# Loading q and k in 32x32 blocks and transposing them on VectorE in place of TensorE

## The chip, the cores and the metric

The kernel runs on one core of one Trainium2 chip. The metric is the device time of one execution in microseconds; three runs of the kernel before gave a median of 990.67.

## The reference

Three stages follow each other. Attention has batch 4, 8 heads, 768 positions and 64 values per head; each position sees the first 4 positions (the sinks) and the last 128. Its output, as 3072 tokens of 512 values, passes a linear stage, and then a mixture of 8 experts of which each token takes one.

```
scores = scale * np.matmul(q, k.transpose(0, 1, 3, 2))
keep = is_sink | in_window
...
a = a / (np.sum(a, axis=-1, keepdims=True) + 1e-09)
x = np.matmul(a, v)            # attention
a = x @ w1; b = x @ w2
x = (a * b @ w3) @ w_out       # linear stage; then routing, and one expert per token
```

## The kernel before

The engines are TensorE (PE, with its weight loads as PEld), VectorE (DVE), ScalarE (ACT), GpSimd (POOL) and SyncE (SP), which issues most of the transfers. Every fp32 matrix product is made of three products of a high and a low part.

**Attention** runs over 48 work items, n = 0 to 47: a unit of 256 positions (12 of them) times a pair of heads (4). In this document an item is one n. For each n, `a_load` brings q and k in (two buffers each), `a_tqk` turns them so that the head's values lie on the partitions, `a_scores` makes scores, maximum and exponential for the two halves j = 0 and 1, `a_pt` and `a_skT` transpose the probabilities, and `a_pv` multiplies them with v. `att_stream` writes these steps in five pieces per item: `a_load(n + 2)` is written ahead of `a_scores(n, 0)`, and `a_tqk(n + 1)` between the two scores steps of n.

**What `a_tqk` does.** Four TensorE transposes (L396) write q and k, turned, into one bank of the PSUM pool `ps_t`. ScalarE copies the bank into `qh` (L401) and into the key store `ring` (L402): the high parts. The low parts are the remainders. For the first 8 items (`n < FEW`) TensorE and ScalarE make them; from n = 8 on VectorE does, `ql` on L413 and the low half of `ring` on L415, with one operand from the PSUM bank and one from SBUF. `ps_t` has one bank, shared by `a_tqk`, `a_pt` and the routing counts (L798 to L802).

**The linear stage** (`moe1_stream`) runs in six groups of two units, beside the attention of the units to come. A group has eight steps f: 24 matmuls (L715), the products `g` on VectorE (L722, L725), and six matmuls with the first unit's half (L703). When the eight are done, the second unit's half follows in eight short steps, the "late" part, beside which attention is written more densely. `route` then works out each unit's experts on VectorE, 16 products of rows with a gate row per unit (L776) and some small steps; `xs<-rows` (L795) stores its rows. The last group's tail and the experts (L924, L961) end the program.

**The order** of instructions on each engine is set by a list scheduler at build time, from the order in which the code is written, with a cost model of its own. Each engine then works strictly in that order. A transfer into a buffer waits on SP until the last reader of the buffer is done, and what stands behind it on SP waits too.

Of the kernel before, what the change touches and what calls it, by code (L numbers as in the profile page):

```python
# [9 lines left out]
F32 = DT.float32  # L10
# [4 lines left out]
ACTF = mybir.ActivationFunctionType  # L15
ALU = mybir.AluOpType
# [6 lines left out]
def f32(ap):  # L23
    return ap.bitcast(F32)
# [3 lines left out]
def attention_moe_moe_kernel(ctx, tc, q, k, v, w1, w2, w3, w_out, mod_id, w_gate, mod_bias, e_w1, e_w2, out,  # L28
                             n_sink, window, dbg=None):
    nc = tc.nc  # L30
    B, H, S, D = q.shape
# [3 lines left out]
    UNIT = 256  # L35
    NC = S // UNIT
    NU = B * NC
    NP = H // 2
# [6 lines left out]
    NS = 4  # L45
    KW = 128 + NS
    banded = n_sink == NS and window == 128
    QDIV = float(D) ** 0.5
    FEW = 2 * NP if math.frexp(QDIV)[0] == 0.5 else 0

    const = ctx.enter_context(tc.tile_pool(name="const", bufs=1))
# [14 lines left out]
    ps_t = psum_ctx.enter_context(tc.tile_pool(name="ps_t", bufs=1, space=PSUM))  # L66
# [3 lines left out]
    att = att_ctx.enter_context(tc.tile_pool(name="att", bufs=2, side="right"))  # L70
# [4 lines left out]
    def defer(fn):  # L75
        job = [fn]

        def run():
            if job:
                job.pop()()  # L80

        waiting[1].append(run)
        return run
# [11 lines left out]
    idf = const.tile([128, 128], F32, name="idf")  # L95
# [19 lines left out]
    def consts_early():  # L115
# [5 lines left out]
        nc.vector.tensor_scalar(out=neg_r, in0=idf, scalar1=-1.0, scalar2=None, op0=ALU.mult)  # L121
        nc.vector.tensor_scalar(out=negq_r, in0=idf, scalar1=-QDIV, scalar2=None, op0=ALU.mult)
        nc.gpsimd.memset(tmp, 1.0)
# [216 lines left out]
    nat = {}  # L340
# [4 lines left out]
    def a_load(n):  # L345
        u, p = divmod(n, NP)
        b, c = divmod(u, NC)
        hs = slice(2 * p, 2 * p + 2)
        qn = att.tile([128, 2, 2 * D], F32, tag="qn", bufs=2, name="qn")
        kn = att.tile([128, 2, 2 * D], F32, tag="kn", bufs=2, name="kn")  # L350
        for src, dst in ((q, qn), (k, kn)):
            for j in range(2):
                s0 = c * UNIT + j * 128
                nc.sync.dma_start(out=dst[:, j].rearrange("p (h d) -> p h d", h=2),
                                  in_=src[b, hs, s0:s0 + 128, :].rearrange("h s d -> s h d"))
        nat[n] = (qn, kn)

    def a_load_v(n):
        u, p = divmod(n, NP)
# [23 lines left out]
    def a_tqk(n):  # L383
        u, p = divmod(n, NP)
        b, c = divmod(u, NC)
        qn, kn = nat.pop(n)
        if n < NP:
            ring.append(att.tile([128, 2, 3, KW], F32R, tag=f"ring{p}", bufs=1, name="ring"))
        kr = ring[p]
        s0, s1 = 2 * c % 3, (2 * c + 1) % 3  # L390
        blocks = slice(s0, s1 + 1) if s0 < s1 else slice(s1, s0 + 1, s0 - s1)
        tp = ps_t.tile([128, 4, 128], F32, tag="t", name="tqk")
        for x, src in enumerate((qn, kn)):
            for j in range(2):
                i = j if x == 0 or s0 < s1 else 1 - j
                nc.tensor.matmul(out=tp[:, 2 * x + i], lhsT=src[:, j], rhs=idf, is_transpose=True, start=(x + j == 0),  # L396
                                 stop=(x + j == 2), skip_group_check=True)
        qh = att.tile([128, 2, 128], F32R, tag="qh", bufs=2, name="qh")
        ql = att.tile([128, 2, 128], F32R, tag="ql", bufs=2, name="ql")
        scale = 1.0 / float(D) ** 0.5  # L400
        nc.scalar.activation(out=qh, in_=tp[:, 0:2], func=ACTF.Copy, scale=scale)  # L401
        nc.scalar.activation(out=kr[:, 0, blocks, NS:KW], in_=tp[:, 2:4], func=ACTF.Copy)  # L402

        def low_parts():
            if n < FEW:
                nc.tensor.matmul(out=tp[:, 0:2], lhsT=negq_r, rhs=qh, start=False, stop=True, skip_group_check=True)
                nc.tensor.matmul(out=tp[:, 2:4], lhsT=neg_r, rhs=kr[:, 0, blocks, NS:KW], start=False, stop=True,
                                 skip_group_check=True)
                nc.scalar.activation(out=ql, in_=tp[:, 0:2], func=ACTF.Copy, scale=scale)
                nc.scalar.activation(out=kr[:, 1, blocks, NS:KW], in_=tp[:, 2:4], func=ACTF.Copy)  # L410
                sinks()
                return
            nc.vector.scalar_tensor_tensor(out=ql, in0=tp[:, 0:2], scalar=scale, in1=f32(qh), op0=ALU.mult,  # L413
                                           op1=ALU.subtract)
            nc.vector.tensor_tensor(out=kr[:, 1, blocks, NS:KW], in0=tp[:, 2:4], in1=f32(kr[:, 0, blocks, NS:KW]),  # L415
                                    op=ALU.subtract)
            sinks()

        def sinks():
            if c == 0:  # L420
                nc.gpsimd.tensor_copy(out=kr[:, :, :, 0:NS],
                                      in_=f32(kr[:, :, 0, NS:2 * NS]).unsqueeze(2).to_broadcast([128, 2, 3, NS]))

        stt["low", n] = defer(low_parts)
        stt["q", n] = (qh, ql)

    def a_scores(n, j):
# [38 lines left out]
        def norm():  # L466
            r = st[:, 2]
            nc.vector.tensor_scalar(out=st[:, 1], in0=st[:, 1], scalar1=1.0e-9, scalar2=None, op0=ALU.add)
            nc.vector.reciprocal(out=r, in_=st[:, 1])
            if n < FEW:  # L470
                for h in range(2):
# [57 lines left out]
    def a_pv(n):  # L529
# [11 lines left out]
        for x, (vj, cols, pm) in enumerate(spans):  # L541
            for h in range(2):
# [3 lines left out]
        nc.tensor.matmul(out=xp[:, 0, j0 * 128:256], lhsT=stt["vsk", b][:, p, :], rhs=sk[:, j0 * 128:256],  # L546
                         start=False, stop=n >= FEW, skip_group_check=True)
        xh, xl = xb[:, p, 0, u % 3], xb[:, p, 1, u % 3]
        nc.scalar.activation(out=xh, in_=xp[:, 0], func=ACTF.Copy)
        if n < FEW:  # L550
            nc.tensor.matmul(out=xp[:, 0], lhsT=neg_r, rhs=xh, start=False, stop=True, skip_group_check=True)
# [10 lines left out]
    def att_stream():  # L562
        a_tqk(0); yield
        a_load(1)
        a_load_sinks(0)
        a_vsink(0)
        yield
        for n in range(NN):
            if n + 2 < NN:
                a_load(n + 2)  # L570
            a_scores(n, 0); yield
            if n:
                a_load_v(n)
                a_sk(n - 1); a_pt(n - 1); yield
            if n + 1 < NN:
                a_tqk(n + 1)
            if n:
                a_skT(n - 1)
            yield
            a_scores(n, 1); yield  # L580
            if n:
                a_pv(n - 1)
                att_done[0] = n
                if n % (NP * NC) == 0:
                    a_vsink(n // (NP * NC))
            yield
        a_sk(NN - 1); a_pt(NN - 1); yield
        a_skT(NN - 1)
        a_pv(NN - 1)
        att_done[0] = NN  # L590
        yield
# [413 lines left out]
    def front():  # L1005
# [19 lines left out]
        if banded:  # L1025
            a_load(0)
            a_load_v(0)
# [202 lines left out]
```

## Time and profile before

| | |
|---|---|
| median of three runs | 990.67 us (990.64 to 991.0) |
| the profiled execution | 990.5 us |
| its span, first to last instruction | 988.5 us |
| PE busy | 955.5 us (97%) |
| DVE busy | 634.0 us (64%) |
| ACT busy | 442.1 us (45%) |
| POOL busy | 161.0 us (16%) |
| mean granted TensorE clock | 0.993 |

The profiled execution was 2.0 us longer than its span. Busy time is the union of an engine's instructions. PE's matmuls overlap each other in the records, so the mean duration of one is longer than the distance from one start to the next.

### The profile page before, as it was taken

Reading aid. Unit: us, or ns where it says so; the run is one execution under the profiler, and the core shown is the slowest. Engines: PE = TensorE matmul, PEld = TensorE weight load, DVE = VectorE, ACT = ScalarE, POOL = GpSimd, SP = SyncE. Lnnn points to the kernel's source line nnn. Section 1 sums busy time; section 2 is a strip of 40 time slices with the busy share of each in tenths; the row PEclk is TensorE's granted clock in tenths of the full one; section 3 lists DMA queues with packets and bytes.
Section 4 is the critical chain, followed back from the end, with each engine's and each line's share of the span. In section 5 each row is a group of like instructions: output and inputs, shape, how many; then the busy total and the mean of one; then the engine's idle time right before and its main releaser. Section 6 shows DMA issues by size and latency. Waiting matters only on the chain. (4 is left out here: it accounts for less than half of the span.)

```text
span 988.5 us, 15433 instructions
## 1 busy us (share of the span) xinstructions
PE 955.5 (97%) x5000; PEld 728.4 (74%) x5000; DVE 634.0 (64%) x1913; ACT 442.1 (45%) x1266; POOL 161.0 (16%) x237
## 2 busy tenths in 40 slices
PE   4899999999999999999999999999999999999995
PEld 3667777767776777677767776787888888888884
DVE  7956994599449953995499538939934373443432
ACT  3687763454335433553355335413434334433433
POOL 1111110111112111111111111123130312211010
PEclk9899999999999999999999999999999999999998
DMA  8754724122212221221022210422455465444331
GB/s 255 237 159 137 224 73 124 29 54 62 46 28 46 64 46 25 51 73 42 19 54 69 47 23 10 138 76 55 141 180 115 150 78 167 149 144 135 106 121 51
DMA packets 125409, 93.99 MB, mean 95 GB/s; under 512 B 96711, under 2 KB 105159, under 8 KB 125200
## 3 DMA queue, kind: packets, MB, share of 16 engines
q1 hardware_dynamic: 120560, 80.12, 30.2%
q0 software_dynamic: 4768, 12.88, 4.1%
q8 instruction: 40, 0.66, 0.3%
q14 instruction: 41, 0.34, 0.2%
HBM read 80.14 MB, written 13.09 MB: 94 GB/s over the span
## 5 line engine op out<-in xcount | busy, mean ns | idle before, releaser
L715 PE MATMUL ab<-xb,wab 128*128 128x512 f32 x1152 | 288.5, 397 | 0.0
L715 PEld LDWEIGHTS ab<-xb,wab 128*128 128x128 f32 x1152 | 209.9, 188 | 44.6 <-DVE xb L554 0.2
L961 PE MATMUL x<-w 128*128 128x512 f32 x600 | 141.0, 392 | 0.0
L776 DVE CUSTOM_DVE_ANT_0 junk<-rows,wgb 128x512 bf16<-128x512 f32 x192 | 137.0, 714 | 1.9 <-ACT rows L763 0.5
L703 PE MATMUL x2p<-w3o,gh 128*128 128x512 f32 x384 | 130.1, 416 | 0.5 <-ACT gh L692 0.5
L961 PEld LDWEIGHTS x<-w 128*128 128x128 f32 x600 | 111.6, 188 | 23.1 <-DVE w L201 0.4
L524 POOL TENSOR_SCALAR_AFFINE_SELECT ptp<-ptf 128x512 f32<-128x512 f32 (+1 forms) x96 | 63.6, 687 | 344.9 <-ACT ptf L519 344.9
L463 ACT ACTIVATE P<-sp,st 128x132 f32<-128x132 f32 (+1 forms) x192 | 69.2, 366 | 67.6 <-DVE st L461 62.4
L201 DVE TENSOR_TENSOR w<-wst,w 128x512 fp32r<-128x512 f32 x112 | 71.3, 685 | 10.8 <-ACT w L200 10.8
L703 PEld LDWEIGHTS x2p<-w3o,gh 128*128 128x128 f32 x384 | 65.7, 189 | 16.2 <-ACT gh L692 2.8
L703 PE MATMUL x2p<-w3o,gl 128*128 128x512 f32 x192 | 76.5, 399 | 0.0
L722 DVE TENSOR_TENSOR g<-ab,bs 128x256 f32<-128x256 f32 x48 | 20.3, 423 | 85.6 <-PE tqk L396 49.0
L924 PE MATMUL ab<-w,w 128*128 128x512 f32 x288 | 74.9, 395 | 0.0
L928 DVE SCALAR_TENSOR_TENSOR w<-ab,w 128x512 fp32r<-128x512 f32 x48 | 33.1, 690 | 64.4 <-ACT w L927 64.2
L924 PE MATMUL ab<-w 128*128 128x512 f32 x288 | 73.6, 391 | 0.0
L692 ACT ACTIVATE gh<-g 128x256 fp32r<-128x256 f32 x96 | 39.7, 415 | 73.8 <-DVE g L722 55.7
L200 ACT ACTIVATE w<-wst 128x512 fp32r<-128x512 f32 x112 | 63.3, 628 | 7.4 <-DMA wst<-in_moe_w_dram 7.2
L443 PE MATMUL sp<-ring,qh 64*128 64x264 f32 (+1 forms) x384 | 62.7, 331 | 3.6 <-ACT P L463 3.5
L924 PEld LDWEIGHTS ab<-w,w 128*128 128x128 f32 x288 | 53.9, 188 | 12.4
L924 PEld LDWEIGHTS ab<-w 128*128 128x128 f32 x288 | 54.1, 188 | 12.1
L443 PEld LDWEIGHTS sp<-ring,qh 64*128 64x128 f32 x384 | 37.5, 185 | 34.6 <-issue 15.1
L927 ACT ACTIVATE w<-ab 128x512 fp32r<-128x512 f32 x48 | 28.7, 597 | 71.8 <-PE ab L924 71.4
(201 smaller groups left out, 1430.8 us busy)
## 6 DMA issues: line engine op xcount, KB each, us to landing
wst<-in_moe_w_dram SPq DMA_DIRECT2D x56, 512.0 KB
f64st<-in_moe_w_dram SPq DMA_DIRECT2D x32, 512.0 KB
vn<-in_v_dram SPq DMA_DIRECT2D x128, 64.0 KB
xs<-rows SPq DMA_DIRECT2D x12, 513.0 KB
qn<-in_q_dram SPq DMA_DIRECT2D x96, 64.0 KB
kn<-in_k_dram SPq DMA_DIRECT2D x96, 64.0 KB
f64st<-in_moe_w_out_dram SPq DMA_DIRECT2D x8, 512.0 KB
wgb<-wgt SPq DMA_DIRECT2D x1, 2048.0 KB
```

The costliest lines, as they stand in the source:

```text
L200: nc.scalar.activation(out=hi, in_=src, func=ACTF.Copy)
L201: lo_eng.tensor_tensor(out=lo, in0=src, in1=f32(hi), op=ALU.subtract)
L443: nc.tensor.matmul(out=sp[:, h, 0:nk].rearrange("p (a b) -> p a b", b=KW), lhsT=a[hp, j, :], rhs=kr[hp, b_, blocks, :], start=(i == 0), st ...
L463: nc.scalar.activation(out=P[:, j, h, lo:KW], in_=sp[:, h, lo:KW], func=ACTF.Exp, bias=st[:, 0, h:h + 1], accum_out=st[:, 1, h:h + 1])
L524: nc.gpsimd.affine_select(out=parts[:, a, i0:2].rearrange("p j h q -> p (j h) q"), in_=full[:, 2 * i0:4], pattern=[[0, 4 - 2 * i0], [sign, ...
L692: nc.scalar.activation(out=gh, in_=g, func=ACTF.Copy)
L703: nc.tensor.matmul(out=x2p[t], lhsT=a[:, sl], rhs=b_, start=(f == 0 and i == 0), stop=(f == KF - 1 and i == 2))
L715: nc.tensor.matmul(out=bank[nm].rearrange("p (u t) -> p u t", u=2), lhsT=a, rhs=b_, start=(kk == 0 and i == 0), stop=(kk == KD - 1 and i = ...
L776: nc.vector.tensor_tensor_reduce(out=junk, in0=rows[:, t, 0:DM], in1=wgb[0][:, e, :], scale=1.0, scalar=0.0, op0=ALU.mult, op1=ALU.add, ac ...
L924: nc.tensor.matmul(out=hp, lhsT=a[:, fs], rhs=b_, start=(kk == 0 and i == 0), stop=(kk == KD - 1 and i == 2))
L928: nc.vector.scalar_tensor_tensor(out=h[:, 1], in0=hp, scalar=0.0, in1=f32(h[:, 0]), op0=ALU.max, op1=ALU.subtract)
L961: nc.tensor.matmul(out=op, lhsT=a[:, ts], rhs=b_, start=(f == 0 and i == 0), stop=(f == KF - 1 and i == 2))
```

## The change

From n = 8 on (`BY_PE`), q and k are loaded in blocks. Partition group g (32 partitions) holds 32 of a head's 64 values, and the 256 positions lie in eight blocks of 32 columns. One transfer moves 32 partitions x 8 blocks x 32 values, with runs of 128 bytes; an item takes eight such transfers in place of four with runs of 256 bytes. A VectorE transposition of [128, 512] then turns each 32x32 block in place, and the copies and the low parts read that SBUF tile instead of the PSUM bank. The first eight items are unchanged except for the tile's name.

```
+    BY_PE = 2 * NP
...
+        qk = att.tile([128, 2, UNIT], F32, tag="qk", bufs=2, name="qk")
...
+            for g in range(4):
+                h, d0 = 2 * p + g // 2, g % 2 * 32
+                nc.sync.dma_start(out=qk[g * 32:(g + 1) * 32, x].rearrange("p (b i) -> p b i", i=32),
+                                  in_=src[b, h, c * UNIT:(c + 1) * UNIT, d0:d0 + 32].rearrange("(b s) i -> s b i", s=32))
...
-        tp = ps_t.tile([128, 4, 128], F32, tag="t", name="tqk")
-        for x, src in enumerate((qn, kn)):
-            for j in range(2):
-                i = j if x == 0 or s0 < s1 else 1 - j
-                nc.tensor.matmul(out=tp[:, 2 * x + i], lhsT=src[:, j], rhs=idf, is_transpose=True, start=(x + j == 0),
-                                 stop=(x + j == 2), skip_group_check=True)
...
+        else:
+            nc.vector.transpose(out=qk.rearrange("p x s -> p (x s)"), in_=qk.rearrange("p x s -> p (x s)"))
+            qt, kt = (qk[:, x].rearrange("p (j s) -> p j s", j=2) for x in range(2))
+            if s0 > s1:
+                kt = kt[:, ::-1]
...
+        nc.scalar.activation(out=qh, in_=qt, func=ACTF.Copy, scale=scale)
+        nc.scalar.activation(out=kr[:, 0, blocks, NS:KW], in_=kt, func=ACTF.Copy)
...
-            nc.vector.scalar_tensor_tensor(out=ql, in0=tp[:, 0:2], scalar=scale, in1=f32(qh), op0=ALU.mult,
+            nc.vector.scalar_tensor_tensor(out=ql, in0=qt, scalar=scale, in1=f32(qh), op0=ALU.mult,
                                            op1=ALU.subtract)
-            nc.vector.tensor_tensor(out=kr[:, 1, blocks, NS:KW], in0=tp[:, 2:4], in1=f32(kr[:, 0, blocks, NS:KW]),
+            nc.vector.tensor_tensor(out=kr[:, 1, blocks, NS:KW], in0=kt, in1=f32(kr[:, 0, blocks, NS:KW]),
                                     op=ALU.subtract)
```

Line numbers of the changed kernel are 13 or 14 higher behind these edits: L443 is L456 there, L715 is L728, L776 is L789; the transposition is L407 and the block load L360.

The scheduler makes a new order for the whole program. On PE, in the last step f of the second group, the order before has the item's transposes between the weight products (`ab`) and the transposes of the sinks' probabilities (`skn`):

```order
L715 MATMUL ab<-xb,wab 128x512 x12
L515 MATMUL pt<-idf,P 128x128 x4
L715 MATMUL ab<-xb,wab 128x512 x12
L396 MATMUL tqk<-idf,qn 128x128 x2
L396 MATMUL tqk<-idf,kn 128x128 x2
L499 MATMUL xp<-idf,skn 8x128 x2
```

The changed kernel has at the same place:

```order
L728 MATMUL ab<-xb,wab 128x512 x12
L528 MATMUL pt<-idf,P 128x128 x4
L728 MATMUL ab<-xb,wab 128x512 x12
L512 MATMUL xp<-idf,skn 8x128 x2
L716 MATMUL x2p<-w3o,gh 128x512 x2
```

The two `tqk` rows are gone, and the rest stands as before. Over the program 160 transposes leave PE.

On DVE, at the change from a late part to the next group's first step (the first such place), the order before has an item's two low parts (`ql`, `ring`) next to each other, behind the mask and the maximum of another half (`sp`, `st`):

```order
L455 COPY_PREDICATED sp<-past_i,sp 128x2x128
L475 TENSOR_TENSOR P<-P,st 128x264
L461 TENSOR_REDUCE st<-sp 128x2
L413 SCALAR_TENSOR_TENSOR ql<-tqk,qh 128x256
L415 TENSOR_TENSOR ring<-tqk,ring 128x2x128
L504 TENSOR_TENSOR pskT_107<-xp,pskT_107 8x256
```

The changed kernel has, at the same place, the low parts of one item apart, and the transposition of the next item behind them:

```order
L426 SCALAR_TENSOR_TENSOR ql<-qk,qh 128x256
L481 TENSOR_SCALAR st<-st 128x2
L567 TENSOR_TENSOR xb<-xp,xb 128x256
L482 RECIPROCAL st<-st 128x2
L706 TENSOR_TENSOR gl<-g,gh 128x256
L488 TENSOR_TENSOR P<-P,st 128x264
L468 COPY_PREDICATED sp<-cur_i,sp 128x2x128
L428 TENSOR_TENSOR ring<-qk,ring 128x2x128
L474 TENSOR_REDUCE st<-sp 128x2
L798 TENSOR_REDUCE sm<-wk 128x2
L804 TENSOR_REDUCE sm<-wk 128x2
L407 STREAM_TRANSPOSE qk<-qk 128x512
```

Each item's transposition stands after the low part `ql` of the item two before, whose buffer it uses. In dense attention some 39 rows stand between the two, four products `junk` among them; beside the steps f about ten rows, with one product `g` among them. Routing is moved too: between the eighth `g` of a group and the first of the next, 22, 22, 21 and 22 products `junk` stood in the first four gaps, and 20, 18, 18 and 20 stand there now, with three transpositions in each gap; the rest of the routing stands behind the next one to three `g`, together with one transposition in each of these steps.

On SP, the order before alternates the loads of q, k and v, with the stores `xs` between them:

```order
L354 DMA qn<-in_q_dram 128x2x64 x2
L354 DMA kn<-in_k_dram 128x2x64 x2
L795 DMA xs<-rows 128x2x513
L365 DMA vn<-in_v_dram 128x2x64 x3
L354 DMA qn<-in_q_dram 128x2x64 x2
```

The changed kernel has there:

```order
L360 DMA qk<-in_q_dram 32x8x32 x4
L360 DMA qk<-in_k_dram 32x8x32 x4
L808 DMA xs<-rows 128x2x513
L360 DMA qk<-in_q_dram 32x8x32 x4
L360 DMA qk<-in_k_dram 32x8x32 x4
```

Eight issues stand where four did; the sequence of items and stores is otherwise alike, with some loads of v moved by one place.

## Rows read from the trace of the kernel before

**Rows 1.** The page: engines, and VectorE's busy tenths in 40 slices
```profile
PE 955.5 (97%) x5000; PEld 728.4 (74%) x5000; DVE 634.0 (64%) x1913; ACT 442.1 (45%) x1266; POOL 161.0 (16%) x237
...
DVE  7956994599449953995499538939934373443432
```

**Rows 2.** Busy time by stretch (`x`: instructions): A, late parts
```profile
core 0: us, PE busy (x) PEld busy (x) DVE busy (x) ACT busy (x) POOL busy (x), PEclk, DMA share, GB/s
192.60:231.50 38.90, 37.93 (x222) 25.58 (x220) 36.90 (x133) 22.73 (x86) 4.89 (x10) 1.00 0.26 61
...
494.20:532.80 38.60, 37.63 (x221) 25.50 (x219) 36.82 (x132) 22.81 (x86) 5.04 (x10) 1.00 0.26 62
sum 160.10, PE 156.44 PEld 106.29 DVE 150.09 ACT 94.09 POOL 23.77; mean PE 39.11 PEld 26.57 DVE 37.52 ACT 23.52 POOL 5.94
```

**Rows 3.** The same view: sums of B (three steps f each) and C
```profile
sum 99.80, PE 99.80 PEld 76.85 DVE 75.74 ACT 34.69 POOL 13.81; mean PE 24.95 PEld 19.21 DVE 18.93 ACT 8.67 POOL 3.45
...
sum 141.30, PE 141.30 PEld 109.30 DVE 58.83 ACT 46.89 POOL 22.72; mean PE 35.33 PEld 27.32 DVE 14.71 ACT 11.72 POOL 5.68
```

**Rows 4.** The same view of L396 alone: busy (matmuls), one A, one B
```profile
192.60:231.50 38.90, 2.90 (x20) 1.00 0.26 61
231.50:257.00 25.50, 0.87 (x7) 1.00 0.20 56
```

**Rows 5.** Busy time by stretch, columns as in group 2: ahead of A, and its fullest part
```profile
88.00:150.00 62.00, 61.86 (x353) 45.56 (x354) 58.73 (x134) 42.73 (x123) 8.94 (x16) 1.00 0.52 149
...
200.00:225.00 25.00, 24.08 (x148) 16.19 (x147) 24.56 (x90) 14.25 (x57) 3.40 (x7) 1.00 0.27 61
```

**Rows 6.** Waits from 150 to 608 us: total us, times, longest
```profile
PEld tqk L396 <- ACT ptf L519: 2.4, 7, 0.5
...
PEld tqk L396 <- ACT ptp L521: 1.8, 5, 0.4
```

**Rows 7.** Timeline of PE around one item's four transposes: start, us
```profile
403.65 0.38 PE L396 MATMUL tqk<-idf,qn 128*128 128x128 f32 x2
403.87 0.38 PE L396 MATMUL tqk<-idf,kn 128*128 128x128 f32 x2
404.09 0.38 PE L499 MATMUL xp<-idf,skn 128*8 128x128 f32 x2
```

**Rows 8.** VectorE instructions by line: ns min/median/max; first and last start
```profile
L752 DVE STREAM_TRANSPOSE wgst<-wgst x1: 692/692/692, 145.4 to 145.4; 32x512 f32<-32x512 f32 x1
...
L380 DVE TENSOR_TENSOR vsk<-vst,vsk x3: 683/683/684, 185.5 to 484.2; 32x512 fp32r<-32x512 f32 x3
...
L201 DVE TENSOR_TENSOR w<-wst,w x112: 675/684/757, 635.3 to 975.0; 128x512 fp32r<-128x512 f32 x112
...
L413 DVE SCALAR_TENSOR_TENSOR ql<-tqk,qh x36: 401/414/425, 162.7 to 607.8; 128x256 fp32r<-128x256 f32 x36
...
L693 DVE TENSOR_TENSOR gl<-g,gh x73: 401/420/901, 157.0 to 604.5; 128x256 fp32r<-128x256 f32 x73
```

**Rows 9.** Groups by line, 150 to 608 us: busy, mean ns of one
```profile
L693 DVE TENSOR_TENSOR gl<-g,gh 128x256 fp32r<-128x256 f32 x73 | 31.9, 438 | 6.6 <-ACT gh L692 6.1 <-PE tqk L396 0.3
...
L524 POOL TENSOR_SCALAR_AFFINE_SELECT ptp<-ptf 128x512 f32<-128x512 f32 x48 | 35.5, 763 | 170.9 <-ACT ptf L519 170.9
```

**Rows 10.** SP's issues by line: ns min/median/max; first and last start
```profile
L354 SPq DMA_DIRECT2D kn<-in_k_dram x96: 391/460/1605, 2.7 to 577.6; - x96
...
L374 SPq DMA_DIRECT2D vst<-in_v_dram x24: 250/295/372, 28.0 to 326.1; - x24
```

**Rows 11.** Timeline of SP: the last two issues of one item's loads
```profile
312.51 0.93 SPq L354 DMA_DIRECT2D kn<-in_k_dram  x2
```

**Rows 12.** Busy time behind those issues, columns as in group 2
```profile
312.00:315.00 3.00, 3.00 (x18) 2.26 (x17) 3.00 (x11) 1.92 (x7) 0.99 (x1) 1.00 0.39 87
315.00:316.00 1.00, 1.00 (x5) 0.47 (x3) 0.94 (x5) 0.65 (x4) 0.20 (x1) 1.00 0.00 0
```

**Rows 13.** SP's waits from 150 to 608 us: total us, times, longest
```profile
SPq L795 <- DVE rows L794: 33.1, 6, 23.7
```

More of the change, by code (lines that the diff above doesn't have):

```diff
@@ L348, in a_load @@
         hs = slice(2 * p, 2 * p + 2)
-        qn = att.tile([128, 2, 2 * D], F32, tag="qn", bufs=2, name="qn")
-        kn = att.tile([128, 2, 2 * D], F32, tag="kn", bufs=2, name="kn")
-        for src, dst in ((q, qn), (k, kn)):
-            for j in range(2):
[L353 to L356, printed above, removed]
+        qk = att.tile([128, 2, UNIT], F32, tag="qk", bufs=2, name="qk")
+        for x, src in enumerate((q, k)):
+            if n < BY_PE:
+                for j in range(2):
+                    s0 = c * UNIT + j * 128
+                    nc.sync.dma_start(out=qk[:, x, j * 128:(j + 1) * 128].rearrange("p (h d) -> p h d", h=2),
+                                      in_=src[b, hs, s0:s0 + 128, :].rearrange("h s d -> s h d"))
+                continue
+            for g in range(4):
+                h, d0 = 2 * p + g // 2, g % 2 * 32
+                nc.sync.dma_start(out=qk[g * 32:(g + 1) * 32, x].rearrange("p (b i) -> p b i", i=32),
+                                  in_=src[b, h, c * UNIT:(c + 1) * UNIT, d0:d0 + 32].rearrange("(b s) i -> s b i", s=32))
+        nat[n] = qk
     def a_load_v(n):
@@ L385, in a_tqk @@
         b, c = divmod(u, NC)
-        qn, kn = nat.pop(n)
+        qk = nat.pop(n)
         if n < NP:
@@ L391, in a_tqk @@
         blocks = slice(s0, s1 + 1) if s0 < s1 else slice(s1, s0 + 1, s0 - s1)
-        tp = ps_t.tile([128, 4, 128], F32, tag="t", name="tqk")
-        for x, src in enumerate((qn, kn)):
-            for j in range(2):
-                i = j if x == 0 or s0 < s1 else 1 - j
-                nc.tensor.matmul(out=tp[:, 2 * x + i], lhsT=src[:, j], rhs=idf, is_transpose=True, start=(x + j == 0),
-                                 stop=(x + j == 2), skip_group_check=True)
+        if n < BY_PE:
+            tp = ps_t.tile([128, 4, 128], F32, tag="t", name="tqk")
+            for x in range(2):
+                for j in range(2):
+                    i = j if x == 0 or s0 < s1 else 1 - j
+                    nc.tensor.matmul(out=tp[:, 2 * x + i], lhsT=qk[:, x, j * 128:(j + 1) * 128], rhs=idf, is_transpose=True,
+                                     start=(x + j == 0), stop=(x + j == 2), skip_group_check=True)
+            qt, kt = tp[:, 0:2], tp[:, 2:4]
+        else:
[3 more added lines that the diff above has]
+                kt = kt[:, ::-1]
         qh = att.tile([128, 2, 128], F32R, tag="qh", bufs=2, name="qh")
@@ L400, in a_tqk @@
         scale = 1.0 / float(D) ** 0.5
-        nc.scalar.activation(out=qh, in_=tp[:, 0:2], func=ACTF.Copy, scale=scale)
-        nc.scalar.activation(out=kr[:, 0, blocks, NS:KW], in_=tp[:, 2:4], func=ACTF.Copy)
+        nc.scalar.activation(out=qh, in_=qt, func=ACTF.Copy, scale=scale)
+        nc.scalar.activation(out=kr[:, 0, blocks, NS:KW], in_=kt, func=ACTF.Copy)
         def low_parts():
```

## The prediction, made before the changed kernel was run

> **What bounds the kernel now.** I read the page first. TensorE is busy for 97% of the span and VectorE for 64%, but in the 40 slices VectorE has groups of one to three that are full [rows 1]. Those groups recur with the linear stage's groups, so I cut the stretch from 192.6 to 593.8 us at the products `g` (L722) and asked for busy times there. A is the 39 to 42 us of each late part, from the eighth `g` of a group to the first of the next. B is the next three steps f, C the last four. Over four groups A took 160.1 us, with TensorE at 156.4 and VectorE at 150.1 [rows 2]: both are nearly full. B took 99.8 us and C 141.3 us; TensorE has no idle time in either, and VectorE works 75.7 and 58.8 us of them [rows 3]. So TensorE's work sets the pace of B and C, and in A it is a close race. Of 48 items, q and k of 36 (n = 12 to 47) are transposed between 150 and 608 us, by their windows five of a group's eight in A (20 matmuls) and nearly two in B (7) [rows 4], so one in C. Items 8 to 11 lie in 88 to 150 us, where VectorE is busy for 58.73 of 62 us [rows 5].
>
> The waits say what part of TensorE's little idle time belongs to the change: the transposes of q and k waited 2.4 + 1.8 us until ScalarE had emptied the shared bank [rows 6].
>
> **What the change removes.** 160 transposes leave TensorE. Their durations overlap, so I price the distance of starts: 403.65 us for the first two, 403.87 for the next two, 404.09 for what follows, so 0.44 us for four and 0.11 us for one [rows 7]. For the 36 items that is 15.8 us. The four items in 88 to 150 us I price at nothing, since VectorE sets the pace there; 1.8 us is their upper bound. The waits for the bank, 4.2 us, go with the transposes. As the next user of TensorE inherits part of them, I take 2 us, between 0 and 4.2.
>
> **What it adds on VectorE.** Forty transpositions of [128, 512]. The trace has one of [32, 512], which took 692 ns. Whether four times the partitions cost more, it does not show for this operation. For a subtraction of 512 columns it does: 683 ns on 32 partitions and 684 (median) on 128 [rows 8]. I take 0.69 us. The lower bound is 0.68, the row of the subtraction; the upper one is four times 692 ns, 2.8 us, if the four groups of partitions went one after the other. The low parts now have both operands in SBUF. Their nearest row for that is L693, mean 438 ns [rows 9], against 414 for L413 with one operand in PSUM [rows 8]: 0.024 us more for each, two per item. An item thus adds 0.69 + 0.05 = 0.74 us. ScalarE's two copies per item read SBUF instead of PSUM; ScalarE is busy for 94 of 160 us in A [rows 2], and its idle time covers what they may gain in length. Without that cover they would delay the scores' weight loads.
>
> L693 shows where the 0.024 comes from: median 420, but up to 901 ns, where L413 never exceeds 425 [rows 8]. GpSimd's masks (L524) have a mean of 763 ns [rows 9]. [...] By the rows the 72 low parts lose 72 x 0.024 = 1.7 us of VectorE. [...]
>
> **Does VectorE have room?** The order answers where the work stands: routing is moved out of A (22, 22, 21, 22 products before, 20, 18, 18, 20 now), three transpositions come into each A, and one into each of the three steps of B. So I take A and B together: 259.9 us of time, 225.8 us of VectorE. Added are 24 transpositions and the low parts of 28 items (A and B hold seven of a group's eight), 24 x 0.69 + 28 x 0.05 = 18.0 us: 243.8 us. TensorE's share falls by 28 x 0.44 = 12.3 us, to 247.6. VectorE would then have to be busy for 98.5% of it. In its fullest 25 us it reached 24.56, 98% [rows 5]; over a whole A 36.82 of 38.60, 95.4% [rows 2]. At 98% A and B take 248.8 us (11.1 saved), at 95.4% 255.6 (4.3 saved). I take the middle, 7.7 us saved. The other eight items, in C, the first stretch and the last late part, save their 8 x 0.44 = 3.5 us: in C VectorE is busy for under half. In 88 to 150 us four transpositions add 2.8 us to an engine with 3.3 us idle; I take 1 us lost, between 0 and 2.8.
>
> **The loads.** SP issues eight transfers in place of four. One issue took 0.46 us (median, L354) with 256 runs, and 0.295 with far fewer (L374) [rows 10]; the new one has 256 runs of half the length, so 0.295 to 0.46, and eight take 2.4 to 3.7 us. Before, an item's last loads were issued until 312.51 + 0.93 = 313.44 us [rows 11] and the transfer engines were quiet from 315 on [rows 12], at most 1.6 us later. From the release of a buffer to the data I reckon 5.3 us. The release is later now: not TensorE's transposes but the low part `ql` ends the buffer's use. Behind it the transposition two items later must not come sooner than 5.3 us. In A some 39 rows of VectorE stand between, at the 36.90 us for 133 rows of an A [rows 2] 10.8 us; in C there is one step f, and C's sixteen steps take 8.8 us each [rows 3]. So the loads are covered by at least 3 us, and cost nothing.
>
> **The sum.** 990.5 - 7.7 (A and B) - 3.5 (the rest) - 2 (the bank) + 1 (88 to 150 us) = 978.3 us; I predict 978.0. The profiled execution, 990.5 us with 2.0 us of it outside the span, lies 0.2 us under the median of the three runs, so it stands for them. A difference under 0.2%, about 2 us, is what a measurement of this kernel could not tell from none.
>
> **The rivals.**
>
> *TensorE alone counts.* If VectorE can be filled in A and B, or its idle time there was only waiting for TensorE, the whole 15.8 us come out, and the bank's 4.2 us: 970.5 us. For it: VectorE still has 10 us of idle time in the four A and 24 in B, and routing has slack. Against it: 98.5% of two stretches is more than the trace shows in any A. Chance 0.18 for 964 to 972.
>
> *VectorE becomes the bound of A.* The slower case. If A's five items add 0.74 us each to VectorE without routing really moving out of its way, A's 150.1 + 20 x 0.74 = 164.9 us at 95.4% take 172.9 in place of 160.1, 12.8 us more; B, C and the rest save 16 x 0.44 = 7.0, the bank 2, the start loses 1: 995.3 us. It decides if in A VectorE's time per item rises by more than TensorE's 0.44 us falls. Against it stands the order, which puts two to four products fewer into A. The 2.8 us of a slow transposition would belong here and would give far more: 24 x 2.1 = 50 us. Chance 0.14.
>
> *The loads come late.* Every transposition stands on VectorE in order, so a late load stops everything behind it. If data took 8.8 us from `ql` instead of 5.3, each further 0.35 us on 36 items would cost 12.6 us, and the gain would be gone: about 990 us. What could do it is `xs` on SP, which waited up to 23.7 us for its rows [rows 13], with loads behind it. [...] In 3 us the sixteen transfer engines were busy for 0.39 of the time, 1.2 us, with one item's loads [rows 12]; doubled, 2.4 us, they still fit beside up to 3.7 us of issuing. No run here shows runs of 128 bytes. Chance 0.08, for 988.5 to 992.5.
>
> **How the numbers follow.** My forecast, 972 to 984 us, has 0.50; a small gain, 984 to 988.5, as at the 95.4% with more lost to the ports, 0.10. The likeliest gives 978.0. With the larger gain 0.18, no change 0.08 and slower 0.14, faster by over 0.2% has 0.78. From 964 to 989 us lie 0.78 and a little of the case of no change, so that is the range.
>
> **What would show it.** Right, if TensorE's transposes of q and k end with the eighth item, VectorE's transposition takes about 0.69 us forty times, A is a few microseconds shorter with VectorE above 95%, B hardly shorter, C shorter by about 0.4 us an item, and no VectorE instruction waits for a transfer into `qk`. Wrong, if the transposition takes much longer than 0.7 us, if VectorE waits for `qk`'s transfers, or if TensorE shows new idle time in A behind VectorE's low parts.

## The result, and the profile of the changed kernel

The changed kernel took 975.69 us (median of 4 runs, 974.91 to 976.49), the kernel before 990.67 us on the same chip (4 runs). The ratio is 0.9847, with a 95% interval of 0.9835 to 0.9859: 15.0 us faster. The forecast was 978.0 us. The profiled execution took 976.12 us, of which 974.4 are the span; the span before was 988.5 us, 14.1 us more.

The page, to be laid beside [rows 1]: the engines' busy time, and VectorE's busy tenths in 40 slices.

```profile
PE 936.3 (96%) x4840; PEld 709.8 (73%) x4840; DVE 654.8 (67%) x1953; ACT 450.6 (46%) x1266; POOL 166.7 (17%) x237
...
DVE  6956996699649964997599649939934374333422
```

TensorE has 160 instructions fewer, and VectorE 40 more. TensorE's busy time fell by 19.2 us, from 955.5 to 936.3, but the span fell by only 14.1, so TensorE's idle time rose from 33.0 to 38.1 us. VectorE's full slices stand in pairs, nearly as before; the slices behind the pairs rose from 4 or 5 tenths to 6 or 7. Lines below the edit have moved by 13: `g` is L735 now, the scores are L456, and VectorE's transposition is L407.

Cut at `g` as in the prediction, here are the sums of the four late parts A, with the busy time of each engine (the answer to [rows 2]), of B and of C (the answer to [rows 3]):

```profile
sum 151.40, PE 145.51 PEld 97.43 DVE 143.69 ACT 92.10 POOL 25.77; mean PE 36.38 PEld 24.36 DVE 35.92 ACT 23.02 POOL 6.44
...
sum 99.00, PE 97.84 PEld 74.08 DVE 93.38 ACT 42.02 POOL 11.92; mean PE 24.46 PEld 18.52 DVE 23.34 ACT 10.50 POOL 2.98
...
sum 138.20, PE 138.20 PEld 105.77 DVE 63.19 ACT 48.79 POOL 26.13; mean PE 34.55 PEld 26.44 DVE 15.80 ACT 12.20 POOL 6.53
```

Four late parts went from 160.1 to 151.4 us, four B from 99.8 to 99.0, four C from 141.3 to 138.2. That is 12.6 of the 14 us by which the span is shorter. The rest is 0.7 us up to the first late part (192.6 to 191.9) and 0.7 in the last late part and its products; what follows the last `g` takes the same time. VectorE's work went where the order had put it: B now has 93.4 us of it, not 75.7.

VectorE's new instructions and TensorE's last transposes of q and k, by line: nanoseconds (minimum, median, maximum), first and last start.

```profile
L407 DVE STREAM_TRANSPOSE qk<-qk x40: 691/710/714, 100.3 to 559.1; 128x512 f32<-128x512 f32 x40
...
L426 DVE SCALAR_TENSOR_TENSOR ql<-qk,qh x40: 373/422/551, 109.8 to 583.1; 128x256 fp32r<-128x256 f32 x40
...
L428 DVE TENSOR_TENSOR ring<-qk,ring x40: 403/419/536, 110.2 to 560.4; 128x256 fp32r<-128x256 f32 x40
...
L403 PE MATMUL tqk<-idf,qk x32: 270/273/421, 10.1 to 94.4; 128*128 128x128 f32 x32
```

One transposition of 128 partitions takes 710 ns; [rows 8] have 692 for 32 partitions. The low parts took 3 to 8 ns longer in the median (414 and 416 before), not 24. Waits between 150 and 608 us (us in total, times, longest), first three of TensorE in the kernel before:

```profile
PEld xp L543 <- POOL ptp L524: 2.2, 4, 1.1
...
PEld pt L515 <- issue: 2.0, 8, 0.4
PEld pt L515 <- DVE P L475: 2.0, 3, 0.7
```

The same three in the changed kernel, and two of VectorE:

```profile
PEld xp L556 <- POOL ptp L537: 4.7, 8, 0.8
...
PEld pt L528 <- issue: 4.0, 5, 1.6
PEld pt L528 <- DVE P L488: 3.7, 5, 1.3
DVE qk L407 <- DMA qk<-in_k_dram: 3.6, 2, 2.3
...
DVE qk L407 <- DMA vn<-in_v_dram: 3.0, 2, 1.5
```

TensorE's waits of [rows 6], 4.2 us, are gone, but these three have grown from 6.2 to 12.4 us: for GpSimd's masks, and ahead of the transposes `pt`. All waits of TensorE's weight loads over the whole execution add up to 101.4 us before and 104.5 us in the changed kernel. Four of VectorE's 40 transpositions waited for a transfer; the second row names a load of v, which the transposition does not read, because the profile infers who ended a wait.

### The profile page after: what moved, and what is told of

Its sections match the earlier page's. It is cut to its first block, busy times and chain, and to the rows that moved or that the text cites. A ratio compares the mean times of both kernels' runs of the same rounds, so it can differ in the third digit from the quotient of the medians.

```text
span 974.4 us, 15492 instructions
## 1 busy us (share of the span) xinstructions
PE 936.3 (96%) x4840; PEld 709.8 (73%) x4840; DVE 654.8 (67%) x1953; ACT 450.6 (46%) x1266; POOL 166.7 (17%) x237
## 3 DMA queue, kind: packets, MB, share of 16 engines
q1 hardware_dynamic: 164080, 80.13, 32.1%
## 5 line engine op out<-in xcount | busy, mean ns | idle before, releaser
L728 PE MATMUL ab<-xb,wab 128*128 128x512 f32 x1152 | 289.8, 397 | 0.3 <-DVE g L738 0.3
L728 PEld LDWEIGHTS ab<-xb,wab 128*128 128x128 f32 x1152 | 209.3, 188 | 45.3 <-PE sp L456 0.5
L789 DVE CUSTOM_DVE_ANT_0 junk<-rows,wgb 128x512 bf16<-128x512 f32 x192 | 135.7, 707 | 1.8 <-ACT rows L776 0.9
L537 POOL TENSOR_SCALAR_AFFINE_SELECT ptp<-ptf 128x512 f32<-128x512 f32 (+1 forms) x96 | 68.0, 732 | 317.8 <-ACT ptf L532 317.7
L735 DVE TENSOR_TENSOR g<-ab,bs 128x256 f32<-128x256 f32 x48 | 20.2, 421 | 67.3 <-PE ab L728 52.5
L937 PEld LDWEIGHTS ab<-w,w 128*128 128x128 f32 x288 | 53.9, 188 | 12.4
L456 PE MATMUL sp<-ring,qh 64*128 64x264 f32 (+1 forms) x384 | 60.5, 329 | 1.2 <-ACT P L476 0.8
L456 PEld LDWEIGHTS sp<-ring,qh 64*128 64x128 f32 x384 | 36.5, 185 | 31.9 <-ACT P L476 11.9
```

The costliest lines, as they stand in the source:

```text
L456: nc.tensor.matmul(out=sp[:, h, 0:nk].rearrange("p (a b) -> p a b", b=KW), lhsT=a[hp, j, :], rhs=kr[hp, b_, blocks, :], start=(i == 0), st ...
L537: nc.gpsimd.affine_select(out=parts[:, a, i0:2].rearrange("p j h q -> p (j h) q"), in_=full[:, 2 * i0:4], pattern=[[0, 4 - 2 * i0], [sign, ...
L728: nc.tensor.matmul(out=bank[nm].rearrange("p (u t) -> p u t", u=2), lhsT=a, rhs=b_, start=(kk == 0 and i == 0), stop=(kk == KD - 1 and i = ...
L789: nc.vector.tensor_tensor_reduce(out=junk, in0=rows[:, t, 0:DM], in1=wgb[0][:, e, :], scale=1.0, scalar=0.0, op0=ALU.mult, op1=ALU.add, ac ...
L937: nc.tensor.matmul(out=hp, lhsT=a[:, fs], rhs=b_, start=(kk == 0 and i == 0), stop=(kk == KD - 1 and i == 2))
```

## The experiments

Each kernel was timed beside the kernel before, on the same chip; the third column is that kernel's median in the same series of runs, and the fourth the difference. To compare two experiments of different series, I subtract their differences. An interval of about 0.0013 in the ratio is 1.3 us, so two such differences tell some 2 us apart.

| Kernel | us | before | difference | ratio, 95% interval |
|---|---|---|---|---|
| changed | 975.69 | 990.67 | -15.0 | 0.9835 to 0.9859 |
| e1_no_turn | 973.62 | 991.12 | -17.5 | 0.9812 to 0.9844 |
| e2_second_turn | 975.10 | 991.12 | -16.0 | 0.9823 to 0.9850 |
| e3_pe_kept | 996.34 | 991.12 | +5.2 | 1.0032 to 1.0059 |
| e4_natural_no_turn | 974.08 | 991.12 | -17.0 | 0.9811 to 0.9838 |
| e5_route_held | 977.39 | 990.73 | -13.3 | 0.9851 to 0.9882 |
| e6_route_held_before | 992.90 | 990.73 | +2.2 | 1.0015 to 1.0038 |
| e7_three_turns | 977.12 | 990.73 | -13.6 | 0.9845 to 0.9877 |
| e8_one_pe | 983.00 | 990.73 | -7.7 | 0.9907 to 0.9935 |
| e9_pe_in_scores | 992.35 | 991.13 | +1.2 | 0.9998 to 1.0016 |
| e10_by_pe_12 | 976.72 | 991.13 | -14.4 | 0.9836 to 0.9868 |
| e11_read_sbuf | 1009.11 | 991.13 | +18.0 | 1.0159 to 1.0203 |
| e12_turn_into_bank | 973.70 | 991.16 | -17.5 | 0.9820 to 0.9847 |

### What VectorE's transposition costs: without it, and with more of it

Left out (e1_no_turn):

```diff
-            nc.vector.transpose(out=qk..., in_=qk...)
```

> The changed kernel without VectorE's transposition: the copies and low parts read the blocks as they were loaded, so q and k of 40 items are wrong and the tokens may be routed otherwise; the stretch up to the last g (614.3 us in the changed kernel) is free of that. Theory (TensorE's removed work is the gain, VectorE's added work is absorbed except for a few us in late parts and first steps, where both are nearly full): A and B come down to what TensorE leaves, 12.3 us under before instead of the 9.6 measured, and the start gives back about 1: 4 us faster than the changed kernel, about 972, last g at about 610. Rival 1 (TensorE alone counts, the transposition is hidden everywhere): within 1 us of the changed kernel, 975.7. Rival 2 (VectorE is now the bound of A and B): 24 transpositions of 0.69 us come back until TensorE stops it, 968 or 969, last g at about 607.

It came 2.5 us under the changed kernel: between the theory's 4 and the first rival's 1, and far from the 7 of a VectorE that bounds A and B. The `g` that the expectation calls the last, at 614.3 us, is the first of the sixth group; it came at 611.0 us, and the true last one at 658.2 instead of 661.5. Both are 3.3 us earlier.

Once more (e2_second_turn), as two instructions of 256 columns, which took 436 ns each:

```diff
+            qd = att.tile([128, UNIT], F32, tag="qd", bufs=1, name="qd")
+            for x in range(2):
+                nc.vector.transpose(out=qd, in_=qk[:, x])
             nc.vector.transpose(out=qk..., in_=qk...)
```

> The changed kernel with as much VectorE transposition once more for each of the 40 items: two of 128x256 into a tile of 1 KB per partition that nobody reads, ahead of the true one; the output is unchanged. Some 0.75 us more of VectorE per item. Theory (VectorE is nearly full in late parts, free in C): about the 12 items of the late parts that carry a transposition pay for most of it, 12 x 0.75 = 9 us, C pays nothing: 985. Rival 1 (TensorE alone counts): 976 to 978. Rival 2 (VectorE is the bound of A and B together): 24 x 0.75 = 18 us and 3 more at the start, 994 to 997.

No cost: 1.0 us under the changed kernel, which is less than two such differences can tell apart. The theory's 9 us are refuted. So I tripled the work in place (e7_three_turns):

```diff
-            nc.vector.transpose(out=qk..., in_=qk...)
+            for _ in range(3):
+                nc.vector.transpose(out=qk..., in_=qk...)
```

> The changed kernel with the transposition of each of the 40 items made three times in place; three give the same as one, and the output is unchanged. 1.4 us more of VectorE per item, 56 us in all, nearly the upper price of the prediction (2.8 us per item would be 2.1 more). In the order the routing gives way: 13 to 16 products in a late part, and some in C. Theory as mended (VectorE's work is free until A, B and C together have no room left): 976 to 980. Rival (VectorE's time in A and B decides as soon as they are full, and the second turn only just fitted): 24 x 1.4 = 34 us less the 13 us still idle there, 995 or more.

It cost 1.4 us, which is again less than two such differences can tell apart. The page gives VectorE's busy time:

```profile
PE 937.9 (96%) x4840; PEld 710.4 (73%) x4840; DVE 695.8 (71%) x2033; ACT 449.9 (46%) x1266; POOL 159.1 (16%) x237
```

The expectation counted 56 us more of VectorE, 80 times the length of one transposition. Its busy time rose by 41.0 us, 0.51 us for each. Here it is over four A, four B and four C, in this order:

```profile
sum 148.80, PE 144.36 PEld 96.72 DVE 140.72 ACT 89.57 POOL 20.55; mean PE 36.09 PEld 24.18 DVE 35.18 ACT 22.39 POOL 5.14
...
sum 100.30, PE 99.41 PEld 74.81 DVE 97.48 ACT 41.51 POOL 8.87; mean PE 24.85 PEld 18.70 DVE 24.37 ACT 10.38 POOL 2.22
...
sum 137.40, PE 137.40 PEld 105.23 DVE 92.05 ACT 50.88 POOL 29.06; mean PE 34.35 PEld 26.31 DVE 23.01 ACT 12.72 POOL 7.27
```

The reader is to look at the DVE column: A holds no more than in the changed kernel (140.7 against 143.7), and C went from 63.2 to 92.0. Of the routing's products (L789 in the changed kernel, L790 here) 58 stand in the four A instead of 76, and 17 run in C, where there had been none and VectorE had been idle for more than half of the time.

### Does the time depend on where the routing stands?

The routing at a higher priority, in the changed kernel (e5_route_held) and in the kernel before (e6_route_held_before):

```diff
-            if next(route_q[0], 0) is None:
+            with tc.high_priority(offset=300):
+                more = next(route_q[0], 0) is None
+            if more:
                 return True
```

> The changed kernel with the routing's steps at a higher priority (offset 300), so that 25, 24, 23 and 25 of its products stand in the four late parts instead of 20, 18, 18 and 20; two transpositions stand in each, not three. Nothing else is edited. In sum 21 products more and 4 transpositions fewer in A, some 12 us of VectorE. Theory (the transposition is free because the routing moved out of its way): A now is VectorE's and grows to about 163 us in four, and TensorE loses most of that: 982 to 988. Rival (TensorE alone counts, wherever VectorE's work stands): within 1.5 us of the changed kernel, 975.7.

> The kernel before the change with the same higher priority of the routing: 24, 24, 23 and 24 products in the four late parts instead of 22, 22, 21 and 22, nearly the number of the changed kernel at that priority. Eight products more, 5.5 us of VectorE in A. Theory (a late part full of VectorE pays): 3 to 5 us slower than before, 994 to 996, and the change under this order is worth less than 15 us, some 8. Rival (TensorE alone counts): within 1.5 us of before, 991, and the change is worth the same 15 us under either order.

The one lost 1.7 us against the changed kernel, far from the theory's 6 to 12; the other lost 2.2 against before, between its rival and its theory. The change is worth 15.5 us in this order as well. A, B and C of the changed kernel with the routing held:

```profile
sum 162.40, PE 156.78 PEld 105.74 DVE 155.96 ACT 90.99 POOL 23.09; mean PE 39.20 PEld 26.43 DVE 38.99 ACT 22.75 POOL 5.77
...
sum 90.40, PE 88.72 PEld 67.15 DVE 73.25 ACT 40.35 POOL 19.81; mean PE 22.18 PEld 16.79 DVE 18.31 ACT 10.09 POOL 4.95
...
sum 136.50, PE 136.50 PEld 103.65 DVE 70.31 ACT 49.85 POOL 17.97; mean PE 34.12 PEld 25.91 DVE 17.58 ACT 12.46 POOL 4.49
```

The late parts did grow by 11.0 us, as the theory said, to 162.4. But TensorE did 11 us more of its work in them, and B and C gave back 8.6 and 1.7 us. VectorE was busy for 96% of these late parts, and little was lost, because TensorE had other work in them. The mended theory, that the transposition is free because the routing moves out of its way, falls with this too: what counts is VectorE's time over the whole group.

### TensorE's time, and the turn in the shared bank

TensorE's transposes put back beside the changed kernel, four per item (e3_pe_kept) or one (e8_one_pe, `range(1)`), of the identity, into the shared bank:

```diff
             nc.vector.transpose(out=qk..., in_=qk...)
+            tp = ps_t.tile([128, 4, 128], F32, tag="t", name="tqk")
+            for i in range(4):
+                nc.tensor.matmul(out=tp[:, i], lhsT=idf, rhs=idf, is_transpose=True, ...)
```

> The changed kernel, and beside it TensorE's four transposes for each of the 40 items, of the identity instead of q and k, into the shared bank, where nobody reads them; the output is unchanged. TensorE gets its removed work back, 0.44 us an item, and pt's wait for the bank in part, but not ScalarE's reading of the bank. Theory (TensorE's time is the gain): 40 x 0.44 = 17.6 us come back, 991 to 994, no better than before, with VectorE's work on top. Rival (the gain was mostly that ScalarE's copies no longer hold the shared bank, which four transposes share with pt): at most 4 to 6 us come back, 980 to 982. Rival 2 (in the late parts VectorE now sets the pace and hides TensorE): only the items outside A, 20 x 0.44 = 8.8 us, come back, 984 to 985.

> The changed kernel with one transpose of the identity by TensorE for each of the 40 items, into the shared bank, where nobody reads it; the output is unchanged. With four of them the time rose by 20.6 us, 17.6 by the distance of starts. If TensorE's own time is the whole of that, one costs a quarter, 4.4 to 5.2 us: 980 to 981. Rival (part is the turn-taking of the shared bank, which one transpose brings as well as four): 4.4 and 3 us more, 983. Second rival (a transpose or two more are hidden in TensorE's idle time): under 2 us, 976 to 977.5.

Four cost 20.2 us, more than the theory's 17.6; one cost 7.3, as its first rival said. The three further transposes thus cost 12.9 us for 120, 0.108 us each: the 0.11 us that [rows 7] give for the distance of two starts. A line through the two points leaves 3.0 us, with some 2 us either way, for no transpose at all. The waits for the bank between 150 and 620 us, in e3_pe_kept and then in e8_one_pe, say where they can lie:

```profile
PEld tqk L410 <- ACT ptf L536: 1.9, 5, 0.5
...
PEld tqk L410 <- ACT ptp L538: 1.2, 3, 0.4
...
PEld tqk L409 <- ACT ptf L535: 2.6, 7, 0.5
...
PEld tqk L409 <- ACT ptp L537: 1.1, 3, 0.4
```

One transpose waits for the bank as long (3.7 us) as four do (3.1 us), and as four did before (4.2 us, [rows 6]). To take the bank out, the four transposes went to a free corner of the scores' bank (e9_pe_in_scores):

```diff
         sp = ps_s.tile([128, 2, 512], F32, tag="s", name="sp")
+        if j == 0 and n >= BY_PE:
+            for _ in range(4):
+                nc.tensor.matmul(out=sp[:, 0, 384:512], lhsT=idf, rhs=idf, is_transpose=True, ...)
```

> The changed kernel with TensorE's four transposes of the identity for each of the 40 items, as in the run that kept them, but written to columns of the scores' bank that nobody uses, ahead of the scores, so that the shared bank has no further user. The output is unchanged. The runs with four and with one transpose in the shared bank gave 20.6 and 7.3 us, as 0.11 us for each transpose and 2.9 us that do not grow with their number. Theory (the 2.9 us are the turn in the shared bank): 17.6 us and no more, 993 to 993.6. Rival (they are no matter of the bank, but of the order or of T beside them): the same 20 us, 996.

Here the same work cost 16.2 us, 4.0 less than in the shared bank and nearer to the theory's 17.6 than to the rival's 20. So the part of TensorE's own time is some 16 us, near the 17.6 of 160 times 0.11, and a turn in the bank costs 3 to 4 us more. The transposes also stand at another place of the order in this run, so a part of the 4.0 may be the order's.

### The loads, and the first four items

The loads as before the change, without the transposition (e4_natural_no_turn), to be compared with e1_no_turn:

```diff
-            if n < BY_PE:
+            if True:
                 for j in range(2):
...
-            nc.vector.transpose(out=qk..., in_=qk...)
```

> The kernel without the transposition, and with the loads as before the change, four transfers of 256-byte runs instead of eight of 128-byte ones; the rest as changed, q and k of 40 items are wrong. Against the kernel with block loads and no transposition it prices the loads. Theory (the block loads are covered): the two differ by under 1.5 us. Rival (the doubled issues on SP or the shorter runs delay items): this one is faster by 3 us or more, about 968.

It was 0.5 us slower than with the block loads, which is nothing: doubled issues and half-length runs cost no time here that the runs can tell. The loads of k did come later in this run, and ScalarE waited for them between 140 and 620 us, where in e1_no_turn it waited 0.2 us:

```profile
ACT ring L414 <- DMA qk<-in_k_dram: 25.8, 12, 5.9
```

Items 8 to 11 turned by TensorE again (e10_by_pe_12, `BY_PE = 3 * NP`):

> The changed kernel with items 8 to 11 turned by TensorE as before (the bound at 12 instead of 8); the output is unchanged. It tests the 88 to 150 us, where the prediction took 1 us of loss (0 to 2.8). Theory (VectorE sets the pace there): 1 us gained, 974.5. Rival (there too TensorE's time counts): 4 x 0.44 = 1.8 us lost, 977.5.

0.6 us slower than the changed kernel: it does not tell the two apart, and the gain that VectorE's full stretch from 88 to 150 us had led me to expect does not show.

### Reading SBUF instead of the bank

Before the change, with TensorE's transposes in place but not used (e11_read_sbuf):

```diff
+        qt, kt = (tp[:, 0:2], tp[:, 2:4]) if n < FEW else (qn, kn if s0 < s1 else kn[:, ::-1])
...
-        nc.scalar.activation(out=qh, in_=tp[:, 0:2], func=ACTF.Copy, scale=scale)
-        nc.scalar.activation(out=kr[:, 0, blocks, NS:KW], in_=tp[:, 2:4], func=ACTF.Copy)
+        nc.scalar.activation(out=qh, in_=qt, func=ACTF.Copy, scale=scale)
+        nc.scalar.activation(out=kr[:, 0, blocks, NS:KW], in_=kt, func=ACTF.Copy)
```

> The kernel before the change, with TensorE's transposes in their place, but from the ninth item on the copies and low parts read the loaded tiles in SBUF and not the bank; q and k of 40 items are wrong. It has TensorE's whole work, no transposition on VectorE and no block loads: what is left of the change is that ScalarE and VectorE read SBUF, and that no copy holds the shared bank. The kept transposes in the changed kernel gave 5.7 us more than before, of which the turn on VectorE explains about 2. Theory (VectorE's transposition, which stands in the chain from the loads to the scores, makes up the rest): within 1 us of before, 991. Rival (the operands in SBUF cost): 993 to 995. Second rival (the copies' hold on the bank was worth something): 987 to 989.

18.0 us slower, which none of the three had foreseen. The longest new wait is one of ScalarE, from 130 to 680 us:

```profile
ACT ring L403 <- DMA kn<-in_k_dram: 48.0, 20, 8.0
```

ScalarE's copies now stand directly behind the loads and ahead of other work. A late load holds ScalarE's queue for up to 8.0 us. Behind it stand the exponentials, and TensorE's scores wait for those (22.0 us for `P` from 190 to 620 us, against 9.6 in the kernel before). That is likely the greater part of the loss, but it is not shown: e4_natural_no_turn has half of ScalarE's wait and lost nothing. So this run says nothing on the price of SBUF operands.

The question was put the other way round with the transposition written to the bank (e12_turn_into_bank):

```diff
-            nc.vector.transpose(out=qk..., in_=qk...)
-            qt, kt = (qk[:, x].rearrange("p (j s) -> p j s", j=2) for x in range(2))
+            tp = ps_t.tile([128, 4, 128], F32, tag="t", name="tqk")
+            nc.vector.transpose(out=tp.rearrange("p a s -> p (a s)"), in_=qk.rearrange("p x s -> p (x s)"))
+            qt, kt = tp[:, 0:2], tp[:, 2:4]
```

> The changed kernel with VectorE's transposition written into the shared bank instead of SBUF; ScalarE's two copies and VectorE's two low parts then read the bank, as before the change, and a buffer of the loads is free as soon as it is turned. The output is unchanged. TensorE has no transposes; the bank has its second user again, worth 2.9 to 4.0 us by the runs with TensorE's transposes in it or beside it. The changes measured one by one (16.7 us of TensorE, 4.0 of the bank, 2.1 of the turn) leave 3.6 us by which the change gave less than they add up to. Theory (those are the reads of SBUF by ScalarE and VectorE): 975.7 + 4.0 - 3.6 = 976, within 1 us of the changed kernel. Rival (SBUF as source costs nothing, the 3.6 us lie in the order): 979 to 980. Second rival (a bank held by VectorE's turn, ScalarE and VectorE at once costs pt more than TensorE's transposes did): 983 or more.

It came 2.5 us under the changed kernel, below all three expectations. Its ratio to before is 0.9833 (0.9820 to 0.9847), the fastest of the versions that compute the whole reference; the interval overlaps that of the changed kernel, so the 2.5 us are likely, not certain. VectorE's waits in it:

```profile
DVE tqk L408 <- ACT ptf L533: 18.4, 15, 2.7
DVE tqk L408 <- ACT ptp L535: 6.9, 4, 2.6
```

And TensorE's, from 150 to 608 us:

```profile
PEld pt L529 <- issue: 2.0, 4, 1.1
PEld pt L529 <- DVE P L489: 1.7, 4, 0.9
PEld xp L557 <- POOL ptp L538: 1.2, 2, 0.6
```

The shared bank has its second user again, and VectorE waits for it for 25 us. That costs nothing that shows, since VectorE has the time; TensorE takes no turn of its own for q and k. The three waits of TensorE that had grown in the changed kernel are 7.5 us shorter here (12.4 against 4.9), while its wait for `P` in the scores grew by 3.5 (9.4 to 12.9). Which of three things brings the gain (sources in the bank, buffers of the loads free one step sooner, or the order that follows) is not settled.

## Why the prediction was right, point by point

**TensorE's transposes.** 0.11 us each, from the distance of starts: right. The runs with one and with four give 0.108. The 270 ns that the profile gives for one transpose would have made 43 us of the 160.

**The waits for the bank.** Taken as 2 us gained, between 0 and 4.2. A turn put back into the bank cost 3.0 and 4.0 us. But in the changed kernel itself the doubt behind the 2, that the next user inherits the wait, is borne out in full: 4.2 us of waits went, and in sum TensorE's weight loads waited 3.1 us longer than before (104.5 against 101.4).

**VectorE's price per item.** As the length of a record, the transposition took 0.71 us against 0.69 taken; the bound of 2.8 us is far off, and its length hardly differs between 32 and 128 partitions (692 and 710 ns). No run shows the loss to ports that the chance of a small gain names; what the runs show is that the low parts took 0.003 to 0.008 us longer in the median, not 0.024, and 551 ns at the longest, against 425 in [rows 8]. Whether GpSimd's masks take longer beside low parts that read SBUF stays open: from 150 to 608 us the mean of a 128x512 mask rose from 763 to 798 ns. Over masks of all widths, from 190 to 620 us, the mean is 694 ns before and 621 in e12_turn_into_bank, where the low parts read the bank; it is 729 in the changed kernel, but anywhere between 644 and 754 in six other runs whose low parts read SBUF (e7_three_turns and e1_no_turn the ends).

**Does VectorE have room? This step failed.** It found VectorE at 98.5% of A and B, took a late part's share of 95.4 or 98% for a ceiling on both together, and charged 4.6 of their 12.3 us for that. Two things were wrong in it. First, VectorE's added work was counted by the length of a record. The sum put 18.0 us into A and B. The 24 transpositions came, and none of the routing's 128 products left these stretches, but VectorE's busy time there rose by only 11.2 us, from 225.8 to 237.1. Records of VectorE overlap in the trace where instructions follow each other without a wait, here by 0.08 to 0.09 us:

```profile
223.99 0.42 DVE L468 COPY_PREDICATED sp<-cur_i,sp 128x256 f32<-128x256 int32 x1
224.32 0.71 DVE L407 STREAM_TRANSPOSE qk<-qk 128x512 f32<-128x512 f32 x1
224.95 0.39 DVE L474 TENSOR_REDUCE st<-sp 128x2 f32<-128x264 f32 x1
```

From the transposition's start to the next one are 0.63 us, and over the whole kernel VectorE's busy time rose by 20.8 us for 40 transpositions, 0.52 us each. The length of a record was thus too high a price; the distance of starts, by which the prediction priced TensorE, is nearer here too. Second, the work in A and B is not fixed. A second and a third turn cost between -1.0 and +1.4 us, and with three of them part of the routing ran in C. Over A and B together VectorE was busy for 94.7% in the changed kernel, 96.7% with a second turn and 95.6% with three, so a ceiling at 98% is not refuted; it was not reached, because the room to count was that of the whole group. VectorE works 300 of the 389 us of A, B and C in the changed kernel, and 330 of 387 with three turns. Leaving the one transposition out gained 2.5 us, so up to some 2.5 us is what it costs; the runs do not resolve it further. Of the prediction's signs of being wrong, new idle time of TensorE did come, from 3.7 to 5.9 us in A and from 0 to 1.2 in B, but none of its waits is for a low part. The rival that TensorE alone counts had the mechanism, and the forecast the better number.

**Which items lie where.** A and B saved 9.5 us, where the sum had 7.7 and a part of the bank. C saved 3.1, where one item for each C would have given 1.8. The count was wrong: [rows 4] count a transpose that lies across a cut in both stretches. The same view for one C, and the starts of transposes around it; one item is four of them:

```profile
257.00:292.50 35.50, 1.20 (x10) 1.00 0.18 27
...
256.95 0.38 PE L396 MATMUL tqk<-idf,kn 128*128 128x128 f32 x2
274.40 0.38 PE L396 MATMUL tqk<-idf,qn 128*128 128x128 f32 x2
...
292.23 0.38 PE L396 MATMUL tqk<-idf,qn 128*128 128x128 f32 x2
```

The ten of this C are two items, at 274.4 and 292.2 us, and the end of one that started in B. By their starts each of the four groups has four items in A, two in B and two in C, where the prediction had five, nearly two and one. At 0.44 us an item that makes 10.6 us for A and B and 3.5 for C, near the 9.5 and 3.1 that they saved.

**88 to 150 us.** One us lost was taken. With four items given back to TensorE the time did not fall. The first `g` comes 2.3 us later than before (133.7 against 131.4), but eight more of TensorE's products (L715) had started by then, 36 instead of 28, and the first group's steps are 3.0 us shorter.

**The loads.** Cost nothing, as predicted; an issue took 448 ns in the median, within the 295 to 460 taken. That no VectorE instruction waits for them was too strong, and it was one of the prediction's signs of being wrong: 6.6 us in four places. VectorE has the time; in e2_second_turn it waits 17.6 us for transfers at the added transpositions, without loss.

**The sum.** 16.2 us of TensorE and 4.0 of the bank, less 2.5 for VectorE's transposition, make 17.7; measured were 15.0. The 2.7 us between are of the size that e12_turn_into_bank wins back, and about what these differences can be added up to. The trace offers a plainer count, an estimate from [rows 7] and the waits: 17.6 us for 160 transposes, less the 3.1 us by which TensorE's waits grew, make 14.5. That 978.0 came within 2.3 us is in part luck, because errors of opposite sign nearly cancel. The sum charged 5.6 us for a full VectorE (4.6 in A and B, 1 at the start) and left out 1.8 us of TensorE's transposes in 88 to 150 us; but it also took 2 us as gained from waits that grew by 3.1.

## What to carry to other kernels

Where work can be moved between stretches, a full engine in one of them is not yet a bound: count its room over the whole period in which the work may be placed, and look for the engine that has none there. Price a short instruction by the distance of starts where records overlap, on VectorE (here 0.63 us, with a record of 0.71) as on TensorE (0.11, with a record of 0.27), and count apart what taking a turn in a shared buffer costs: here one transpose per item waited 3.7 us in sum and four waited 3.1. Look at starts where a cut through a profile may run through an instruction. If someone must wait for a shared buffer, the engine with idle time is worth trying; e12_turn_into_bank agrees with that but does not show it alone.

## What was not expected of the hardware

VectorE's transposition of 128x512 took nearly the same time into PSUM as into SBUF: a mean of 721 ns into the bank in e12_turn_into_bank and 707 in SBUF in the changed kernel (436 ns for 128x256 in SBUF, e2_second_turn). ScalarE's copies of q, 128x256, took a mean of 416 ns from SBUF in the changed kernel and 384 from the bank before. The block loads raised the packets of the hardware queue from 120,560 to 164,080, but its share of the transfer engines' time only from 30.2 to 32.1%; e11_read_sbuf, with the old loads, has 120,560 packets and 29.5%.
